# Gated mix of two attention blocks: the gate formed in the output's stage, mixed output weights stored one at a time, and five staging places for the second half of v

## The chip, the cores and the metric

The kernel runs on one core of one Trainium2 chip. The metric is device time in microseconds (us), the median of several runs of the whole program. TensorE is called PE, VectorE DVE, ScalarE ACT, GpSimd POOL; SP is the engine from whose queue this kernel issues all its DMAs, and the queue is worked off in the order in which the program was written.

## What is computed

One input x (2048 tokens of 1024) goes through two attention blocks with 32 heads of 32, and a gate per token mixes the results:

```python
g = sigmoid((x * gate_w).sum(-1, keepdims=True))
# A, linear attention: phi(t) = where(t > 0, t + 1, exp(t)) + 1e-6
kv = einsum("bhsd,bhse->bhde", phi(k), v); z = einsum("bhsd->bhd", phi(k))
a = (phi(q) kv / (phi(q) z + 1e-6)) @ A_wo
# B, softmax attention
b = softmax(q k^T * 32**-0.5) v @ B_wo
out = g * a + (1 - g) * b
```

All of it is in float32. A float32 product is made of three PE passes: each operand is split into a high part (a cast on ACT, L252) and a low part (a subtraction on DVE or POOL, L253), and high*high, high*low and low*high are added up in one PSUM bank (L146 to L148).

## The kernel before, in words

The program is written out by a planner. It keeps a modelled clock for each engine (`T`, advanced by `use`), several generators ("streams") that yield where they could go on, and a list of small DVE jobs that may be put off (`defer`, `fill`). At every step it takes the stream whose next work can start first or that is furthest behind. The instructions of each engine, and those of SP, then run on the chip in the order in which they were written; an engine waits wherever its next instruction has to.

There are 16 blocks of 128 tokens. The work comes in these stages:

- The first stage makes v's first half and all of B's q and k, and puts the parts of x away in DRAM (`xs`), from where blocks of x come back later.
- `linear()` then runs units of 24 matmuls, one unit for a block of tokens and 512 output columns: 16 units for v's second half ("v"), 64 for block A: keys and values ("kv", 64 units, 256 columns of each), then queries ("q") and outputs ("o") in 32 units each. Unit n reads x from one of two tiles, and the loads for unit n+2 (L583, two DMAs of 512 KB) are issued when unit n has ended.
- `maxima()` makes scores once for the row maxima (L902 on PE, L907 on DVE), beginning during v's second half; `heads_()` makes them again transposed, with the exponential (L1053 on PE, L1057 on ACT) and the sums with v (L1149). These two are interleaved with the units of `linear()`. All of them take their results from a ring of six PSUM banks.
- In stage "q" the keys' sums are multiplied into A's output weights (`mix()`, L669): four times, for two halves of the rows and two of the columns. `load_mix()` (L652) fetches four tiles of A's weights (1 MB) at units 2 and 8 of "q" and again of "o". A mix yields four results; each gives a high part (in the same four tiles, `mix_hi`, slices of `big12`) and a low part (`mix_lo`: `mid7`, `mid10`, `mid0`, `mid1`), and both go out to DRAM (`wa_d`, L679), eight DMAs of 256 KB. The destination of one such DMA is four pieces of 32 rows.
- `output()` takes B's weights and the finished heads, splits them (`split_o`), makes the last product block of tokens by block of tokens (`out_pe`), adds A's part `ra` and stores (`out_done`, L1227 and L1228). Tokens' results wait in a ring of five tiles, each with B's heads in its left half and `ra` in its right half. The last head's rows come into these tiles by five small DMAs (L1202) from `mid11`.

What the change touches: the gate is formed by `gate()` in the v units. For each block two DMAs bring x (L334) into quarters of `big20`, and two DVE instructions (L344) multiply them with the gate's weights (`zrep`, loaded by the program's first DMA, L329) and add them up; behind the last block five short instructions (L346 to L350) make g and 1-g of all blocks at once. g then multiplies the queries' results in `divide` (L824), and 1-g the output in `out_done`. `v_out` (L365 and L366) copies a v unit's bank on ACT into `mid10` or `mid11`, in turns, and stores it. In the first score pass, head 0 and head 1 of q, k and v are loaded in units 0 and 1 (`load_head`: L861, L873; `load_v`: L886).

Of the kernel before, what the change touches and what calls it, by code (L numbers as in the profile page):

```python
# [9 lines left out]
F32 = mybir.dt.float32  # L10
F32R = mybir.dt.float32r
AF = mybir.ActivationFunctionType
ALU = mybir.AluOpType
# [32 lines left out]
def kernel(  # L46
# [32 lines left out]
    def f32(ap):  # L79
        return ap.bitcast(F32)  # L80
# [28 lines left out]
    zrep = sb.tile([P, D], F32, name="zrep")  # L109
    g_sb = sb.tile([P, NT], F32, name="g_sb")  # L110
    omg_sb = sb.tile([P, NT], F32, name="omg_sb")
    tg = sb.tile([P, 2, NT], F32, name="tg")
    mx = [sb.tile([P, NT, NJ], F32, name=f"mx{i}") for i in range(2)]
    mneg = [sb.tile([P, NT], F32, name=f"mneg{i}") for i in range(2)]
    mh = sb.tile([NT, P], F32R, name="mh")
# [38 lines left out]
    def use(eng, cost, *after):  # L154

        T[eng] = max(T[eng], *after, 0.0) + cost
        return T[eng] + LATENCY[eng]
# [142 lines left out]
    PAIRS = [(j, j + 1) for j in range(0, NJ, 2)]  # L300
    tmp = f32(big[20])
    s1, u2, u3 = [tmp[:, i * C:(i + 1) * C] for i in range(3)]
    gate_x = [tmp[:, i * C:(i + 1) * C] for i in range(4)]

    def xop(name, p, i):
        return big[XO[name][p]][:, i * C:(i + 1) * C]
# [19 lines left out]
        nc.tensor.matmul(bank[7][:, :P], ones, ones, start=True, stop=True)  # L326

    HD = D // 2
    nc.sync.dma_start(zrep, bass.AP(tensor=gate_w.tensor, offset=gate_w.offset, ap=[[0, P], [1, D]]))  # L329

    def gate():
        def load(t):
            for i in range(2):
                nc.sync.dma_start(gate_x[t % 2 * 2 + i], x[t * P:(t + 1) * P, i * HD:(i + 1) * HD])  # L334

        load(0)
        for t in range(NT):
            yield
            if t + 1 < NT:
                load(t + 1)  # L340
            for i in range(2):
                gx = gate_x[t % 2 * 2 + i]
                use("dve", 0.7)
                nc.vector.scalar_tensor_tensor(gx, gx, 1.0, zrep[:, i * HD:(i + 1) * HD], op0=ALU.mult,  # L344
                                               op1=ALU.mult, accum_out=tg[:, i, t:t + 1])
        nc.vector.tensor_add(tg[:, 0], tg[:, 0], tg[:, 1])  # L346
        nc.scalar.activation(tg[:, 0], tg[:, 0], AF.Exp, scale=-1.0)
        nc.vector.tensor_scalar_add(tg[:, 0], tg[:, 0], 1.0)
        nc.vector.reciprocal(g_sb, tg[:, 0])
        nc.vector.tensor_scalar(omg_sb, g_sb, -1.0, 1.0, op0=ALU.mult, op1=ALU.add)  # L350

    def spill(js):

# [10 lines left out]
    def v_out(c, t, ps, va):  # L364
        nc.scalar.copy(va, ps)  # L365
        nc.sync.dma_start(v_d[c][:, t, :], va)  # L366
# [75 lines left out]
        nc.sync.dma_start(qk_d[sec][0][g][:, sl], f32(hi))  # L442
        nc.sync.dma_start(qk_d[sec][1][g][:, sl], f32(lo))

    gating = gate()
    xp_done = set()

    def first_xp(n):
# [197 lines left out]
    mixed = []  # L646
    mix_hi, mix_lo = [], (mid[7], mid[10], mid[0], mid[1])

    def load_mix():
        a, c = mix_todo.popleft()  # L650
        for i in range(HK):
            nc.sync.dma_start(mix_hi[i], a_wo[(a * HK + i) * P:(a * HK + i + 1) * P, c * C:(c + 1) * C])  # L652
        mix_here.append((a, c, T["pe"] + 8.0))
# [7 lines left out]
    def mix():  # L661
        a, c, _ = mix_here.pop()
        need(k_left)
        bs = [take() for _ in range(4)]
        end = use("pe", AV + 0.2)
        for r in range(4):
            rows = slice(r * DH, (r + 1) * DH)
            for i in range(HK):
                nc.tensor.matmul(bank[bs[r]][i * DH:(i + 1) * DH, :], kvb[rows, a * HK + i, :], mix_hi[i][rows, :],  # L669
                                 start=True, stop=True)  # L670
        for r in range(4):
            hi, lo, pb = f32r(mix_hi[r]), f32r(mix_lo[r]), bank[bs[r]]
            at = use("act", 0.5, end)
            nc.scalar.copy(hi, pb)

            def low(_, r=r, hi=hi, lo=lo, pb=pb):
                nc.vector.tensor_sub(lo, pb, f32(hi))
                for p, src in enumerate((hi, lo)):
                    nc.sync.dma_start(wa_d[p][a][c][:, r * DH:(r + 1) * DH, :], f32(src))  # L679
                mixed.append((a, c))  # L680

            give(bs[r], 0.0, [defer(low, at)])

# [37 lines left out]
    def linear():  # L721
        extra = iter(())
        coming_w = deque()
        for n, (i, t) in enumerate(units):
# [7 lines left out]
            ps = bank[b]  # L732
            T["pe"] = max(T["pe"], free[b])
            lin_kind[0] = kind
            if kind in ("q", "o") and c == 0 and t in (2, 8, NT - 2):
                yield lambda: None if mix_here else 0.0
                if t < NT - 2:
                    load_mix()
# [3 lines left out]
            for k in range(NK):  # L742
# [19 lines left out]
                if follow and follow[0] == "o":  # L762
                    if pos == NT - 1:
                        w_left[k].clear()
                        yield lambda: 0.0 if mixed.count((k // HK, follow[1])) == 4 else None
                        load_wa(follow[1], k)
                    continue
                if follow and pos == NT - 2 and k < min(LEAD_W, NK):
# [4 lines left out]
                        coming_w.append(load_w(*follow, k + LEAD_W, LEAD_W + 1))  # L773
            if NT // 2 <= n + 2 < len(units):
                load_xp(n + 2)
            for _ in range(1 + (n == 1) if n < NT else 0):
                next(gating, None)
            extra = iter(())
            e, r = mid[3 + n % 3], mid[6]
            if kind == "v":  # L780
                give(b, use("act", 0.5, T["pe"] + LATENCY["pe"]))
                v_out(c, t, ps, mid[10 + t % 2])
            elif kind == "kv":
                va = mid[7][:, (n % 2) * HC:(n % 2 + 1) * HC]
                yield from keys_alone(n - 2)
# [18 lines left out]
            elif kind == "q":  # L804
# [16 lines left out]

                def divide(_, t=t, e=e, ps=ps, d=d):
                    nc.vector.reciprocal(d, d)
                    nc.vector.scalar_tensor_tensor(  # L824
                        e.rearrange("p (h d) -> p h d", d=DH), ps.rearrange("p (h d) -> p h d", d=DH),
                        g_sb[:, t:t + 1], d.unsqueeze(2).to_broadcast([P, C // DH, DH]),
                        op0=ALU.mult, op1=ALU.mult)

                todo = chain(((sums, 0.63), (scaled, 0.63), (dens, 0.63), (divide, 0.9)), end)
                last.append(todo[-1])  # L830
# [187 lines left out]
    def heads_():  # L1018
# [8 lines left out]
        for h in range(H):  # L1027
# [6 lines left out]
            for t in range(NT):  # L1034
                i = slot(h, t)
                for j in range(NJ):
# [19 lines left out]
                    give(b, end)  # L1056
                    nc.scalar.activation(pr_t[i][:, j * C:(j + 1) * C], bank[b], AF.Exp, scale=SCALE)  # L1057
                    st_done[0] += 1
                    if j == 2 and t == 0 and h + 2 < H:
                        load_q(h + 2)  # L1060
                        load_v(h + 2)
# [142 lines left out]
    def split_o(n, ks):  # L1204
# [3 lines left out]
        xo_ready[n] = use("dve", 0.06 + 1.05 * size, use("act", 0.2 + 0.8 * size, T["pe"]))  # L1208
        split(blocks(dst, 0)[:, ks], blocks(dst, 1)[:, ks], o_part(n, ks), nc.vector)

    def out_pe(n, c, k):
        stat = [blocks(xo_t[n % len(xo_t)], p)[:, k] for p in range(2)]
        sl = slice(c * C, (c + 1) * C)
        if (n, c) not in out_b:
            out_b[n, c] = take()
        b = out_b[n, c]
        for _ in three(bank[b], stat, [wo_part(k, p)[:, sl] for p in range(2)], k):
            use("pe", MM, free[b])
# [13 lines left out]

    def output():
        yield lambda: None if "lin" in streams else 0.0
        early = list(range(min(5, NK - 1)))
        for k in early:
            for c in range(NQC):
# [3 lines left out]
        for n in range(1, NF):  # L1241
# [3 lines left out]
            for k in early:  # L1245
                for c in range(NQC):
                    yield lambda: both(wo_end[k], xo_ready[n], 0.0 if (n, c) in out_b else bank_at())
                    out_pe(n, c, k)
        for n in range(NF):
            for k in range(len(early), NK - 1):  # L1250
                for c in range(NQC):
                    yield lambda: wo_end[k]
                    out_pe(n, c, k)
# [10 lines left out]
        for n in range(NT):  # L1264
            if 2 < n + 1 < NT and n >= NF:
                split_o(n + 1, slice(0, NK))
            for c in range(NQC):
                for k in range(NK - 1 if n < NF else 0, NK):
                    out_pe(n, c, k)
                out_done(n, c)  # L1270
# [118 lines left out]
```

## Time and profile before

| | |
|---|---|
| Time, median of 3 runs | 2906.94 us (2906.63 to 2907.45) |
| The profiled execution's own time | 2906.63 us |
| Its span, first to last instruction | 2904.8 us |
| PE busy | 2847.1 us, 98% of the span |
| DVE, ACT, POOL busy | 2227.9, 1596.8 and 1853.9 us |
| Mean granted TensorE clock | 0.991 |
| DMA | 400.55 MB, mean 138 GB/s |

The span and the time differ by 1.8 us, which lie around the first and the last instruction. In the profile's rows, "x12" is a count, the number in front of it is busy time from the first to the last of the merged instructions, and a bracket such as "[6.37 <-DMA big<-xs]" is the idle time of that engine before the instruction and what ended it. "big<-xs" means that a tile called big (its number is left out) was written from xs. SPq is SP's queue: the time of its rows is that of issuing a DMA, not of the transfer. In rows of windows stand, for each engine, busy time and instruction count, then the granted clock, the mean busy share of the 16 DMA engines, and GB/s.

### The profile page before, as it was taken

What the parts mean: (1) busy time and instruction counts of PE and PEld (TensorE: products, weight loads), DVE (VectorE), ACT (ScalarE), POOL (GpSimd) and SP (SyncE); (2) the same over time, 40 slices, a digit from 0 to 9 for tenths busy, and PEclk for the clock granted to TensorE, in tenths of its full rate; (3) what the DMA queues carried; (4) which work ended last, traced back from release to release, by engine and by line L of the source; (5) the groups of instructions that cost most, each with busy time, mean ns of one, the idle gap of its engine ahead of it and who ended that gap; (6) DMA issues with size and microseconds to landing.
All of it is one profiled execution on the core that took longest, in us unless ns stands there. A gap on an engine that the chain in (4) does not pass through costs nothing.

```text
span 2904.8 us, 44336 instructions
## 1 busy us (share of the span) xinstructions
PE 2847.1 (98%) x15744; PEld 2039.5 (70%) x15744; DVE 2227.9 (77%) x3715; ACT 1596.8 (55%) x2976; POOL 1853.9 (64%) x646
## 2 busy tenths in 40 slices
PE   9999989899999999999999999799999999999999
PEld 7888867666666766666666666467676666766787
DVE  6667638788888888888888888688888887886522
ACT  5334320566676667666666666456666665666410
POOL 1212220488798889987988888468777878785000
PEclk9999999999999999999999999899999999999999
DMA  5957765423332324233323235444455344524542
GB/s 174 291 173 216 243 202 189 156 91 98 99 117 76 93 88 120 89 102 92 117 80 91 88 120 165 157 166 146 146 175 182 112 146 127 153 88 140 171 158 78
DMA packets 302496, 400.55 MB, mean 138 GB/s; under 512 B 92682, under 2 KB 185354, under 8 KB 299146
## 3 DMA queue, kind: packets, MB, share of 16 engines
q1 hardware_dynamic: 302276, 397.73, 44.3%
q8 instruction: 124, 2.03, 0.3%
q14 instruction: 96, 0.79, 0.1%
HBM read 287.57 MB, written 108.79 MB: 136 GB/s over the span
## 4 chain that ended last, share of the span: by engine, by line
PE 94%; DMA 3%; DVE 2%; ACT 0%; issue 0%; SPq 0%; ACTq 0%; DVEq 0%
PE bank L1053 16%; PE bank L902 16%; PE bank L1149 15%; PE bank L146 11%; PE bank L148 10%; PE bank L147 10%; PE bank L430 3%; PE bank L432 3%; PE bank L431 3%; PE bank L472 1%; PE bank L955 1%; PE bank L470 1%; PE bank L471 1%; DMA big<-xs 1%; DMA big<-qk 0%; PE bank L707 0%
## 5 line engine op out<-in xcount | busy, mean ns | idle before, releaser
L1102 POOL TENSOR_TENSOR big<-big,big 128x1536 f32<-128x1536 f32 (+1 forms) x434 | 1556.5, 3586 | 209.0 <-ACT big L1057 186.9
L907 DVE TENSOR_REDUCE mx<-bank 128x1 f32<-128x512 f32 x2048 | 1308.7, 680 | 306.7 <-PE bank L902 301.8
L1057 ACT ACTIVATE big<-bank 128x512 f32<-128x512 f32 x2048 | 1180.1, 601 | 528.1 <-PE bank L1053 457.8
L902 PE MATMUL bank<-big,big 128*128 128x512 f32 x2048 | 804.8, 393 | 21.6 <-DVE mx L907 11.9
L1053 PE MATMUL bank<-big,big 128*128 128x512 f32 x2048 | 810.7, 397 | 2.2 <-ACT big L1057 2.0
L146 PE MATMUL bank<-big,big 128*128 128x512 f32 x1408 | 554.6, 394 | 25.4 <-DMA big<-xs 21.4
L148 PE MATMUL bank<-big,big 128*128 128x512 f32 x1408 | 552.6, 392 | 1.0 <-DMA big<-oA 0.8
L147 PE MATMUL bank<-big,big 128*128 128x512 f32 x1408 | 552.8, 393 | 0.0
L1053 PEld LDWEIGHTS bank<-big,big 128*128 128x128 f32 x2048 | 384.4, 188 | 159.8 <-issue 62.8
L902 PEld LDWEIGHTS bank<-big,big 128*128 128x128 f32 x2048 | 385.9, 188 | 106.4 <-DVE mx L907 12.6
L1149 PE MATMUL bank<-big,mid 128*32 128x512 f32 x4096 | 459.2, 593 | 0.0
L146 PEld LDWEIGHTS bank<-big,big 128*128 128x128 f32 x1408 | 265.8, 189 | 91.2 <-issue 19.2
L1149 PEld LDWEIGHTS bank<-big,mid 128*32 128x32 f32 x4096 | 127.7, 110 | 263.6 <-issue 263.6
L148 PEld LDWEIGHTS bank<-big,big 128*128 128x128 f32 x1408 | 266.0, 189 | 58.5 <-DMA big<-oA 1.2
L147 PEld LDWEIGHTS bank<-big,big 128*128 128x128 f32 x1408 | 265.9, 189 | 55.4
L1111 DVE TENSOR_TENSOR bank<-bank,big 128x512 f32<-128x512 f32 (+1 forms) x434 | 280.2, 646 | 7.6 <-ACT big L1057 5.7
L1098 POOL TENSOR_TENSOR big<-big,big 128x1536 f32<-128x1536 f32 (+1 forms) x31 | 111.6, 3601 | 264.7 <-issue 141.1
L253 DVE TENSOR_TENSOR big<-mid,big 128x512 fp32r<-128x512 f32 x216 | 152.8, 731 | 83.9 <-ACT big L252 83.8
L409 POOL TENSOR_TENSOR mid<-mid,mid 128x512 f32<-128x512 f32 x16 | 20.7, 1291 | 278.3 <-DVE big L253 265.3
L252 ACT CAST big<-mid 128x512 fp32r<-128x512 f32 x216 | 130.2, 624 | 100.9 <-POOL mid L410 55.3
L431 PE MATMUL bank<-big,big 128*128 128x512 f32 x448 | 174.3, 389 | 0.0
L432 PE MATMUL bank<-big,big 128*128 128x512 f32 x448 | 174.3, 389 | 0.0
(102 smaller groups left out, 1949.8 us busy)
## 6 DMA issues: line engine op xcount, KB each, us to landing
big<-xs SPq DMA_DIRECT2D x208, 512.0 KB
qk<-mid SPq DMA_DIRECT2D x128, 256.0 KB
big<-oA SPq DMA_DIRECT2D x64, 512.0 KB
big<-qk SPq DMA_DIRECT2D x96, 256.0 KB
big<-qk SPq DMA_DIRECT2D x384, 64.0 KB
mid<-in_b_wqkv SPq DMA_DIRECT2D x88, 256.0 KB
xs<-big SPq DMA_DIRECT2D x64, 256.0 KB
oA<-mid SPq DMA_DIRECT2D x64, 256.0 KB
```

What stands on the lines that cost most here:

```text
L146: yield nc.tensor.matmul(ps, sh, mh_, start=(kt == 0), stop=False)
L147: yield nc.tensor.matmul(ps, sh, ml_, start=False, stop=False)
L148: yield nc.tensor.matmul(ps, sl, mh_, start=False, stop=(kt == NK - 1))
L431: nc.tensor.matmul(ps, sh, ml_, start=False, stop=False)
L432: nc.tensor.matmul(ps, sl, mh_, start=False, stop=(i == HK - 1))
L902: nc.tensor.matmul(bank[b], q[:, t * P:(t + 1) * P], k[:, j * C:(j + 1) * C], start=True, stop=True)
L907: nc.vector.tensor_reduce(m[:, t, j:j + 1], bank[b], AX.X, ALU.max)
L1053: nc.tensor.matmul(bank[b], k[:, t * P:(t + 1) * P], q[:, j * C:(j + 1) * C], start=True, stop=True)
L1057: nc.scalar.activation(pr_t[i][:, j * C:(j + 1) * C], bank[b], AF.Exp, scale=SCALE)
L1102: nc.gpsimd.tensor_add(lacc[:, :qp], lacc[:, :qp], pr(t)[:, :qp])
L1111: nc.vector.tensor_add(lacc[:, qp:] if t == NT - 1 else l_b[:, :n], l_b[:, :n], src)
L1149: nc.tensor.matmul(av_b[j * DH:(j + 1) * DH, :], v[:, t, :], pr(t)[:, j * C:(j + 1) * C], start=(t == 0), stop=(t == NT - 1))
```

## The change

The gate's stage is gone from the v units. `load_g` and a new `gate(n)` stand in `output()`: x of blocks 0 and 1 is loaded when `linear()` has ended, into `mid8`, `mid9` and `mid7`, `mid10`, the gate's weights ahead of them into `zrep` (which block A has used for something else in between), and `gate(n)` loads x of block n+2 behind its own products. It makes g and 1-g of one block in six short DVE and ACT instructions and multiplies `ra` by g on ACT, over 1024 columns; `divide` no longer multiplies by g. Blocks 0 and 1 are gated ahead of the middle part of the output's products, each later block n+1 ahead of block n's products.

`mix()` in stage "q" no longer issues its eight stores at once: they are put into a queue, `stores`, and `heads_()` issues one at each step of four transposed scores (at j == 1). Whatever is left goes out at once when the next `load_mix()` comes or stage "o" begins. In stage "o" the stores are issued as before. `mixed` now counts eight stores instead of four pairs.

`v_out` uses five tiles in turns, `mid10`, `mid11`, `mid7`, `mid8`, `mid9`.

```diff
-    nc.sync.dma_start(zrep, bass.AP(tensor=gate_w.tensor, offset=gate_w.offset, ap=[[0, P], [1, D]]))
-
-    def gate():
-        def load(t):
-            for i in range(2):
-                nc.sync.dma_start(gate_x[t % 2 * 2 + i], x[t * P:(t + 1) * P, i * HD:(i + 1) * HD])
...
+    stores = deque()
+
     def load_mix():
+        while stores:
+            stores.popleft()()
         a, c = mix_todo.popleft()
...
-            def low(_, r=r, hi=hi, lo=lo, pb=pb):
+            def store(p, src, r=r):
+                nc.sync.dma_start(wa_d[p][a][c][:, r * DH:(r + 1) * DH, :], f32(src))
+                mixed.append((a, c))
+
+            def low(_, hi=hi, lo=lo, pb=pb, store=store):
                 nc.vector.tensor_sub(lo, pb, f32(hi))
                 for p, src in enumerate((hi, lo)):
-                    nc.sync.dma_start(wa_d[p][a][c][:, r * DH:(r + 1) * DH, :], f32(src))
-                mixed.append((a, c))
+                    if lin_kind[0] == "q":
+                        stores.append(lambda p=p, src=src: store(p, src))
+                    else:
+                        store(p, src)
...
+            while kind == "o" and stores:
+                stores.popleft()()
...
-            for _ in range(1 + (n == 1) if n < NT else 0):
-                next(gating, None)
...
-                v_out(c, t, ps, mid[10 + t % 2])
+                v_out(c, t, ps, mid[(10, 11, 7, 8, 9)[n % 5]])
...
-                    nc.vector.scalar_tensor_tensor(
+                    nc.vector.tensor_mul(
                         e.rearrange("p (h d) -> p h d", d=DH), ps.rearrange("p (h d) -> p h d", d=DH),
-                        g_sb[:, t:t + 1], d.unsqueeze(2).to_broadcast([P, C // DH, DH]),
-                        op0=ALU.mult, op1=ALU.mult)
+                        d.unsqueeze(2).to_broadcast([P, C // DH, DH]))
...
+                    if j == 1 and stores:
+                        stores.popleft()()
...
+    gate_x = [(mid[8], mid[9]), (mid[7], mid[10])]
+
+    def load_g(n):
+        if n == 0:
+            nc.sync.dma_start(zrep, bass.AP(tensor=gate_w.tensor, offset=gate_w.offset, ap=[[0, P], [1, D]]))
+        t = t_order[n]
+        for i in range(2):
+            nc.sync.dma_start(gate_x[n % 2][i], x[t * P:(t + 1) * P, i * HD:(i + 1) * HD])
+
+    def gate(n):
+
+        t = t_order[n]
+        g, o = g_sb[:, t:t + 1], omg_sb[:, t:t + 1]
+        for i in range(2):
+            gx = gate_x[n % 2][i]
+            nc.vector.scalar_tensor_tensor(gx, gx, 1.0, zrep[:, i * HD:(i + 1) * HD], op0=ALU.mult,
+                                           op1=ALU.mult, accum_out=tg[:, t, i:i + 1])
+        nc.vector.tensor_add(g, tg[:, t, 0:1], tg[:, t, 1:2])
+        nc.scalar.activation(g, g, AF.Exp, scale=-1.0)
+        nc.vector.tensor_scalar_add(g, g, 1.0)
+        nc.vector.reciprocal(g, g)
+        nc.vector.tensor_scalar(o, g, -1.0, 1.0, op0=ALU.mult, op1=ALU.add)
+        ra = o_ring[n % len(o_ring)][:, D:2 * D]
+        nc.scalar.activation(ra, ra, AF.Copy, scale=g)
+        use("act", 1.4, use("dve", 2.2))
+        if n + 2 < NT:
+            load_g(n + 2)
...
         yield lambda: None if "lin" in streams else 0.0
+        for n in range(NF):
+            load_g(n)
...
         for n in range(NF):
+            gate(n)
...
                 split_o(n + 1, slice(0, NK))
+            if NF <= n + 1 < NT:
+                gate(n + 1)
```

Three places of the order are looked at below. Names are tiles with the number of the buffer: `bank` is PSUM, `mx0` the row maxima, `tg` the gate's sums, `wa` the mixed weights in DRAM, `oA` block A's results in DRAM; a first number says which of several a tile is.

On DVE, where the score maxima begin in v's second half, before:

```order
L253 TENSOR_TENSOR big19_227<-mid13_242,big19_227 128x512
L344 SCALAR_TENSOR_TENSOR big20_228,tg_199<-big20_228,zrep_196 128x512 x6
L907 TENSOR_REDUCE mx0_200<-bank5_248 128x1
L907 TENSOR_REDUCE mx0_200<-bank6_249 128x1
L907 TENSOR_REDUCE mx0_200<-bank0_243 128x1
L907 TENSOR_REDUCE mx0_200<-bank1_244 128x1
```

The same place now:

```order
L253 TENSOR_TENSOR big19_227<-mid13_242,big19_227 128x512
L892 TENSOR_REDUCE mx0_200<-bank5_248 128x1
L892 TENSOR_REDUCE mx0_200<-bank6_249 128x1
L892 TENSOR_REDUCE mx0_200<-bank0_243 128x1
L892 TENSOR_REDUCE mx0_200<-bank1_244 128x1
```

The six products of the gate that stood ahead of the first maximum are gone from there.

On SP, around the second mix of stage "q" (the loads of x for unit 9, the results of unit 6, then the fetch of A's weights), before:

```order
L583 DMA big5_213<-xs0_9_72 128x1024
L583 DMA big5_213<-xs1_9_88 128x1024
L714 DMA oA0_6_101<-mid8_237 128x512
L714 DMA oA1_6_117<-mid9_238 128x512
L652 DMA big12_3828<-in_a_wo 128x512 x4
```

The same place now:

```order
L559 DMA big5_213<-xs0_9_72 128x1024
L559 DMA big5_213<-xs1_9_88 128x1024
L700 DMA oA0_6_101<-mid8_237 128x512
L700 DMA oA1_6_117<-mid9_238 128x512
L657 DMA wa1_0_0_166<-mid0_229 4x32x512
L657 DMA wa0_0_0_162<-big12_3758 4x32x512
L657 DMA wa1_0_0_166<-mid1_230 4x32x512
L632 DMA big12_3758<-in_a_wo 128x512 x4
```

The last three stores of the first mix, which before went out in one piece with the other five, ahead of the loads of x for unit 8, are now right ahead of the second fetch; the second of the three reads the quarter of `big12` that the fetch's last DMA writes.

On SP, ahead of the last head's five small DMAs in the output's stage, now (before, the first five of these rows were not there):

```order
L1202 DMA zrep_196<-in_gate_w 128x1024
L1205 DMA mid8_237<-in_x 128x512
L1205 DMA mid9_238<-in_x 128x512
L1205 DMA mid7_236<-in_x 128x512
L1205 DMA mid10_239<-in_x 128x512
L1171 DMA big8_3751<-oB_127 128x896
L1172 DMA big8_3751<-ra1_171 128x1024
L1184 DMA big8_3751<-oB_127 96x128
L1189 DMA big12_3758<-mid11_240 32x128
```

The gate's weights and x of two blocks, 1.5 MB, now go ahead of the loads of the fifth block and of the last head's rows.

More of the change, by code (lines that the diff above doesn't have):

```diff
@@ L111 @@
     omg_sb = sb.tile([P, NT], F32, name="omg_sb")
-    tg = sb.tile([P, 2, NT], F32, name="tg")
+    tg = sb.tile([P, NT, 2], F32, name="tg")
     mx = [sb.tile([P, NT, NJ], F32, name=f"mx{i}") for i in range(2)]
@@ L302 @@
     s1, u2, u3 = [tmp[:, i * C:(i + 1) * C] for i in range(3)]
-    gate_x = [tmp[:, i * C:(i + 1) * C] for i in range(4)]
     def xop(name, p, i):
@@ L328 @@
     HD = D // 2
-    nc.sync.dma_start(zrep, bass.AP(tensor=gate_w.tensor, offset=gate_w.offset, ap=[[0, P], [1, D]]))
-    def gate():
-        def load(t):
-            for i in range(2):
[L334 to L350, printed above, removed]
     def spill(js):
@@ L443, in qk_out @@
         nc.sync.dma_start(qk_d[sec][1][g][:, sl], f32(lo))
-    gating = gate()
     xp_done = set()
@@ L764, in linear @@
                         w_left[k].clear()
-                        yield lambda: 0.0 if mixed.count((k // HK, follow[1])) == 4 else None
+                        yield lambda: 0.0 if mixed.count((k // HK, follow[1])) == 8 else None
                         load_wa(follow[1], k)
```

## The prediction

> **What bounds the kernel now.** The page comes first: how busy PE is, and what runs beside it.
>
> ```profile
> PE 2847.1 (98%) x15744; PEld 2039.5 (70%) x15744; DVE 2227.9 (77%) x3715; ACT 1596.8 (55%) x2976; POOL 1853.9 (64%) x646
> ```
>
> PE is busy in all but 57.7 us of the span of 2904.8. As the change takes no matmul away, it can win back only what PE waits, and what it loses behind a wait by a slow clock. So the next view is PE's waits, by what ended them:
>
> ```profile
> PE bank L146 <- DMA big<-xs: 21.4, 2, 15.0
> PE bank L902 <- DVE mx L907: 11.9, 1, 11.9
> PE bank L902 <- ACT mid L365: 9.5, 2, 6.8
> PE bank L470 <- ACT big L252: 2.5, 1, 2.5
> PE bank L146 <- DVE big L573: 2.1, 1, 2.1
> ```
>
> Few, long waits, 47.4 us in five rows. The first row is two waits for x in stage "q" (6.4 and 15.0), the second and a part of the third (9.5 - 6.8 = 2.7) lie where v's second half begins, the other part (6.8) and the fifth at its end. The windows right behind these waits show the second loss, the granted clock (the number behind the last engine's count):
>
> ```profile
> 424.50:426.60 2.10, 2.04 (x4) 1.16 (x4) 0.00 (x0) 0.01 (x1) 0.00 (x0) 0.50 0.96 218
> 438.50:446.50 8.00, 8.00 (x29) 6.55 (x30) 7.33 (x14) 0.58 (x1) 0.00 (x0) 0.81 0.66 214
> 534.20:542.20 8.00, 8.00 (x29) 6.52 (x30) 6.01 (x11) 4.58 (x9) 0.85 (x1) 0.82 0.83 164
> 1843.90:1851.90 8.00, 8.00 (x30) 5.34 (x34) 4.75 (x9) 3.06 (x5) 4.45 (x2) 0.76 0.99 335
> 1887.90:1895.90 8.00, 8.00 (x29) 6.51 (x30) 4.90 (x8) 2.58 (x5) 0.00 (x0) 0.73 0.58 212
> ```
>
> A window's length times what is missing to 1.00 is time lost: 1.1, 1.5, 1.4, 1.9 and 2.2 us.
>
> **The change part by part.** *The gate leaves the v units: the first wait goes.* SP's queue, DVE and ACT at the beginning of v's second half (timeline):
>
> ```profile
> 420.07 0.38 SPq L366 DMA_DIRECT2D v<-mid  x1
> 421.91 7.76 SPq L873 DMA_DIRECT2D big<-qk  x12
> 430.38 2.70 SPq L334 DMA_DIRECT2D big<-in_x  x4
> 434.85 0.69 DVE L344 SCALAR_TENSOR_TENSOR big<-big,zrep 128x512 f32<-128x512 f32 x1 [11.07 <-DMA big<-in_x]
> 437.75 4.40 DVE L907 TENSOR_REDUCE mx<-bank 128x1 f32<-128x512 f32 x7
> 423.92 0.58 ACT L365 COPY mid<-bank 128x512 f32<-128x512 f32 x1 [11.35 <-DMA v<-mid]
> ```
>
> x for the gate is queued on SP behind the twelve loads of head 1's k, so it lands late; DVE stands 11.07 us before the gate's product at 434.85, the maxima stand behind it until 437.75, seven in a row, and PE has no bank left. Now the maxima follow directly (first pair of listings of the order). Their operands are not late: no wait of PE for head 0's loads is among its rows. The 2.7 us ahead of it is another queue: ACT's third copy waited 11.35 us for the first store of v, which SP issued at 420.07, behind head 0's loads; with five places the third copy needs no store to have landed. The three new places' last use, B's stores of q and k, stands on SP ahead of head 0's loads. I see nothing that is late next: the whole of 11.9 + 2.7 + 1.1 + 1.5 = **17.2 us** goes. The gate's DVE products, removed with it, lay on no other path.
>
> *The end of v's second half.*
>
> ```profile
> 512.69 7.24 SPq L260 DMA_DIRECT2D mid<-in_a_wqkv  x10
> 521.29 0.81 SPq L334 DMA_DIRECT2D big<-in_x  x2
> 522.80 4.54 SPq L260 DMA_DIRECT2D mid<-in_a_wqkv  x6
> 529.16 2.06 ACT L571 CAST big<-mid 128x512 fp32r<-128x512 f32 x3 [4.93 <-DMA mid<-in_a_wqkv]
> 533.41 0.22 ACT L347 ACTIVATE tg<-tg 128x16 f32<-128x16 f32 x1 [2.19 <-DVE tg L346]
> 534.15 0.79 PE L902 MATMUL bank<-big,big 128*128 128x512 f32 x1 [6.85 <-ACT mid L365]
> 520.00:530.00 10.00, 5.17 (x22) 3.64 (x20) 3.65 (x6) 3.23 (x7) 0.00 (x0) 1.00 0.99 327
> ```
>
> PE waits for block A's weights (2.1), then for a bank that ACT empties only behind the casts of three more weights and the gate's exponential. The exponential's 2.2 us wait goes. The casts wait for weights from transfers that run at 327 GB/s with the engines 0.99 busy; two gate loads of 0.5 MB less ahead of them are 3.1 us at that rate. Together 5.3 of the 9.0 us, and most of the clock's 1.4, are taken as **6.5 us**; the bounds are 2.2 (the transfers' end does not move) and 10.3 (everything).
>
> *The stores one at a time: both waits for x go.*
>
> ```profile
> 1822.00:1829.00 7.00, 7.00 (x32) 5.68 (x31) 5.76 (x12) 5.03 (x9) 6.92 (x2) 1.00 0.27 104
> 1819.30 2.61 SPq L679 DMA_DIRECT2D wa<-big  x1
> 1827.02 2.46 SPq L679 DMA_DIRECT2D wa<-mid  x1
> 1835.75 2.70 SPq L583 DMA_DIRECT2D big<-xs  x2
> 1868.13 2.40 SPq L679 DMA_DIRECT2D wa<-mid  x1
> 1881.61 4.59 SPq L583 DMA_DIRECT2D big<-xs  x4
> ```
>
> From the fifth store on, each holds SP for about 2.5 us, while the DMA engines are 0.27 busy: about four of sixteen carry them. Behind eight of them x for unit 8 is issued at 1835.75 and for unit 10 at 1881.61, where PE had stopped 9 us before. Now three stores lie between unit 7's and unit 8's loads, and single ones elsewhere. x lands some 6 us behind its issue (1881.61 to PE's start at 1887.8, ahead of the fifth window), and a unit of "q" lasts longer than that. So 21.4 + 1.9 + 2.2 = **25.5 us** go; were each load still held up by a store in front, about half would stay, the lower bound 13.
>
> The Trainium skill, "DMA: Bandwidth & Descriptors", section "Rules for kernel authors", says that a DMA whose outermost dimension has size c below 16 runs on at most c DMA engines; this store's has four, and the 0.27 agrees. By that rule spreading the stores out makes none of them shorter, and its section "Queues, rings and completion order" adds that each engine takes its descriptors in order, so a load issued behind a store still waits on those four; that outcome is the third rival.
>
> *A new wait at the second mix.* The second pair of listings of the order has three stores right ahead of the fetch of A's weights. Before, that fetch had a free queue:
>
> ```profile
> 1843.85 0.77 PE L146 MATMUL bank<-big,big 128*128 128x512 f32 x1 [6.37 <-DMA big<-xs]
> 1854.66 1.16 PE L669 MATMUL bank<-big,kvb 32*32 32x512 f32 x32
> ```
>
> PE begins unit 8 at 1843.85 and the mix at 1854.66, 10.8 us later, 8.9 at full clock; the order of PE's work there is unchanged. Now, counted from unit 8's start: x of unit 9 and results of unit 6, 1.5 MB at 335 GB/s, with some 1 us of issue, end at 5.7; three stores of 2.5 us on the same four engines at 13.2; 1 MB of weights behind them, 3.1 us, at 16.3. PE would wait 16.3 - 8.9 = 7.4 us, and lose about 2 by the clock, as behind the wait of 6.4: **9.5 us lost**. The bounds are 0 (the stores overlap the rest) and 12.
>
> *The gate in the output's stage.*
>
> ```profile
> L344 DVE SCALAR_TENSOR_TENSOR big<-big,zrep 128x512 f32<-128x512 f32 x32 | 20.9, 686 | 29.3 <-DMA big<-in_x 29.1
> L252 ACT CAST big<-big 128x1024 fp32r<-128x1024 f32 (+2 forms) x18 | 16.8, 956 | 117.4 <-PE bank L147 91.0 <-DMA big<-mid 26.3
> 2760.00:2780.00 20.00, 20.00 (x90) 16.57 (x89) 4.78 (x6) 2.11 (x2) 0.00 (x0) 1.00 0.55 177
> 2733.68 4.48 SPq L1202 DMA_DIRECT2D big<-mid  x5
> 2739.97 2.40 ACT L252 CAST big<-big 128x128 fp32r<-128x128 f32 x4 [14.13 <-DMA big<-mid]
> 2746.59 2.11 DVE L1227 SCALAR_TENSOR_TENSOR big<-bank,omg_sb,big 128x512 f32<-128x512 f32 x3 [3.91 <-PE bank L148]
> 2724.00:2740.00 16.00, 15.16 (x59) 12.05 (x60) 7.46 (x11) 1.87 (x4) 0.00 (x0) 0.89 0.62 216
> ```
>
> Each block costs DVE two products of 0.69 and four short instructions (estimate 0.8 in all), ACT the exponential's 0.22 and a scaling near the cast's 0.96, and 0.5 MB. A block is 48 matmuls, 10.7 us at 90 in 20 us; in that window DVE is busy for a quarter and ACT for a tenth, so these are hidden, also the wait of DVE for ACT within them, since ring and banks run blocks ahead. The first blocks are tighter: 1.5 MB now precede the last head's rows on SP, 7 us at 216 GB/s. They landed at 2739.97; their casts and subtractions take 0.9, and PE came to them at about 2745.7 (its first result is taken at 2746.59): 4.8 us of slack. **1 us lost** (between 0 and 4).
>
> *The program's start.* SP's first DMA was the gate's weights:
>
> ```profile
> 0.75 0.39 SPq L329 DMA_DIRECT2D zrep<-in_gate_w  x1
> ```
>
> Its issue, 0.4, and a part of its 0.5 MB go: **0.7 us** (0 to 2) of the 2.5 that PE waits for its first operands.
>
> The sum is -17.2 - 6.5 - 25.5 + 9.5 + 1.0 - 0.7 = -39.4 us, against the profiled execution's 2906.6: 2867. That execution lies 0.3 below the median of the three runs, which changes nothing.
>
> **The rivals.**
>
> *No new wait at the second mix.* If the stores drain beside the loads, or the fetch's data wait only for the one store that reads their place, the 9.5 stay: 2858. For it: the fetch before was never waited for at this place. Against it: the 0.27. Chance 0.27.
>
> *Spread stores still hold up x.* Half of the 25.5 stays: 2867 + 13 = 2880. For it: each store takes 2.5 us wherever it is. Against it: a unit leaves more than that. Chance 0.14.
>
> *Slower.* The output's stage could become bound by transfers. A block moves 1.5 MB now (heads, `ra`, result) and 2.0 MB with x. Did this stage get no more than the 138 GB/s that the page has as mean, a block would take 14.8 instead of 10.7 us, and 14 blocks 57 us more: 2867 + 57 = 2924. It decides from 2.0 MB in 10.7 us on, 190 GB/s. Against it: engines only 0.55 busy at 177 GB/s here and 335 GB/s elsewhere. Chance 0.03.
>
> *The change doesn't do what it says* can be left out: the order shows all three edits.
>
> **How the numbers follow.** The forecast has 0.56, the rivals 0.27, 0.14 and 0.03. The time is that of the likeliest, 2867. The range goes down past the second case with all of the end of v's half won (2858 - 3.8, about 2854) and up past the third, with some of the output's bound (2880 + 3): 2854 to 2883. Faster by over 0.2% (5.8 us, about what a measurement of this kernel can tell) is every case but the last; the smallest sum of the lower gains, 17.2 + 2.2 + 13 - 12 - 4 = 16 us, is faster too. 0.95 faster, 0.02 the same, 0.03 slower.
>
> **What would show it.** Among PE's waits: no DVE mx at the first maxima, no DMA big<-xs of over 2 us; ACT's copies of v without a wait for v's stores; at the end of v's half one wait of about 3.5 us; at the second mix a wait of PE for big<-in_a_wo of about 7 us; none by DMA big<-in_x in the output's stage. A time under 2854 would mean that the mix and the end of v's half both cost nothing; over 2883, that waits for x stay in "q", or that new ones came where the order had none.

## The result and the profile after

The changed kernel takes 2873.41 us (median of four runs, 2870.82 to 2873.77) against 2907.19 before (four runs, 2906.63 to 2909.41). The ratio is 0.988, with a 95% interval of 0.9863 to 0.9898: 33.8 us faster. The forecast was 39.4 us. The profiled execution took 2873.77 us, with a span of 2872.0, 32.8 less than before. All that follows is compared with that profiled execution.

The page of the changed kernel, PE and the engines beside it:

```profile
PE 2846.1 (99%) x15744; PEld 2036.8 (71%) x15744; DVE 2239.1 (78%) x3775; ACT 1617.8 (56%) x3007; POOL 1854.1 (65%) x646
```

PE's busy time is the same within 1.0 us. Outside it there are 25.9 us of the span where there were 57.7. So 31.8 of the 32.8 us are waits that went. Only 1.0 is shorter busy time, in which a better clock would show; the forecast had a net 5.8 there. PE's waits after the change, to be held against the five rows of the prediction:

```profile
PE bank L649 <- DMA big<-in_a_wo: 7.5, 1, 7.5
PE bank L146 <- DMA big<-xs: 3.4, 2, 2.0
PE bank L887 <- ACT mid L342: 2.9, 1, 2.9
PE bank L1038 <- ACT big L1042: 2.6, 1, 2.6
PE bank L146 <- ACT big L252: 1.9, 1, 1.9
PE bank L446 <- ACT big L252: 0.8, 1, 0.8
```

The 11.9 us for a maximum (DVE mx) are gone, the two waits for x fell from 21.4 to 3.4, and the two for ACT's copies of v (now L342) from 9.5 to 2.9. The first row is the wait at the second mix. It was forecast at 7.4. SP's queue shows how it comes about (after, timeline):

```profile
1814.04 0.51 SPq L657 DMA_DIRECT2D wa<-mid  x1
1814.61 0.64 SPq L657 DMA_DIRECT2D wa<-big  x1
1815.29 1.82 SPq L657 DMA_DIRECT2D wa<-mid  x1
1817.15 8.91 SPq L632 DMA_DIRECT2D big<-in_a_wo  x4
```

The three stores left over from the first mix stand ahead of the fetch of A's weights, as the order had shown. SP then needs 8.91 us to issue four loads.

What that wait costs in all is seen on PE, before and then after, from the mix (L669, now L649) to the four transposes (L707, now L693):

```profile
1855.75 1.93 PE L1149 MATMUL bank<-big,mid 128*32 128x512 f32 x16
1857.60 0.66 PE L707 MATMUL bank<-ident,mid 128*128 128x128 f32 x4
```

```profile
1829.48 3.79 PE L649 MATMUL bank<-big,kvb 32*32 32x512 f32 x32 [7.53 <-DMA big<-in_a_wo]
1833.20 3.17 PE L1136 MATMUL bank<-big,mid 128*32 128x512 f32 x16
1836.31 0.66 PE L693 MATMUL bank<-ident,mid 128*128 128x128 f32 x4
```

Before, the mix began at 1854.66 and the transposes 2.9 us later. Now they begin 6.8 us after the mix's start, with the same matmuls between. So the second mix costs 7.5 of wait and 3.9 behind it, 11.4 us. These 3.9 lie inside "busy" rows: the row of the mix, 32 matmuls of 0.6 us merged, took 1.16 before and takes 3.79 now, and shows no wait among them.

The windows behind the waits, and one of the output's stage (after):

```profile
509.00:516.00 7.00, 7.00 (x19) 5.53 (x20) 5.44 (x10) 3.89 (x7) 0.00 (x0) 0.59 0.98 202
1829.50:1837.50 8.00, 8.00 (x56) 2.41 (x57) 2.48 (x4) 3.10 (x7) 0.00 (x0) 0.61 0.11 25
1853.50:1859.50 6.00, 5.95 (x28) 5.02 (x29) 4.47 (x7) 2.90 (x6) 3.69 (x1) 1.00 0.66 230
1920.40:1926.40 6.00, 5.97 (x31) 2.60 (x35) 5.00 (x9) 3.72 (x7) 4.70 (x2) 0.72 0.94 317
2760.00:2780.00 20.00, 20.00 (x90) 16.56 (x89) 8.35 (x22) 4.59 (x6) 0.00 (x0) 1.00 0.65 210
```

Length times what is missing to 1.00 gives 2.9, 3.1, 0, 1.7 and 0 us. The last row is the stage that took over the gate: PE is busy in all of the 20 us, while DVE went from 4.78 to 8.35, ACT from 2.11 to 4.59 and the transfers from 177 to 210 GB/s. The gate is hidden there.

### The profile page after: what moved, and what is told of

Read it like the earlier page. It is cut to its first block, busy times and chain, and to the rows that moved or that the text cites. A ratio compares the mean times of both kernels' runs of the same rounds, so it can differ in the third digit from the quotient of the medians.

```text
span 2872.0 us, 44436 instructions
## 1 busy us (share of the span) xinstructions
PE 2846.1 (99%) x15744; PEld 2036.8 (71%) x15744; DVE 2239.1 (78%) x3775; ACT 1617.8 (56%) x3007; POOL 1854.1 (65%) x646
## 4 chain that ended last, share of the span: by engine, by line
PE 96%; DMA 2%; DVE 1%; ACT 0%; issue 0%; SPq 0%; ACTq 0%; DVEq 0%
PE bank L1038 16%; PE bank L887 16%; PE bank L1136 15%; PE bank L146 11%; PE bank L148 11%; PE bank L147 11%; PE bank L407 4%; PE bank L409 4%; PE bank L408 4%; PE bank L446 1%; PE bank L940 1%; PE bank L447 1%; PE bank L448 1%; DMA big<-xs 1%; PE bank L693 0%; PE bank L584 0%
## 5 line engine op out<-in xcount | busy, mean ns | idle before, releaser
L1038 PE MATMUL bank<-big,big 128*128 128x512 f32 x2048 | 810.7, 397 | 2.7 <-ACT big L1042 2.6
L1038 PEld LDWEIGHTS bank<-big,big 128*128 128x128 f32 x2048 | 384.6, 188 | 159.7 <-issue 62.0
```

Of the source, the lines that this page charges most:

```text
L1038: nc.tensor.matmul(bank[b], k[:, t * P:(t + 1) * P], q[:, j * C:(j + 1) * C], start=True, stop=True)
```

## The experiments

The theory was that the gains are separate (gate, v's places, stores) and that the new wait at the second mix comes from the stores ahead of the fetch. The rivals were that the gains hide one another, and that not the place of the stores holds up the loads behind them but their form, four pieces on four DMA engines. Each run is compared with the kernel before on the same chip; ratios come with their 95% interval.

**The gate alone.** The changed kernel with its stores and v's places as before:

```diff
-                    if lin_kind[0] == "q":
+                    if False:
...
-                v_out(c, t, ps, mid[(10, 11, 7, 8, 9)[n % 5]])
+                v_out(c, t, ps, mid[10 + t % 2])
```

> The change with only the gate moved: v's copies take two places, the mixed weights' stores go out eight at a time as before. Theory (the gate's products hold up the first maxima, and its loads the end of v's second half): PE's waits by DVE mx (11.9 us) and most of the end of v's half go, with some clock; PE waits by big<-xs in stage q stay at about 21 us; the 2.7 us by ACT's copy stay or shrink. Time 2884 to 2890 us. Rival (the places of v and the stores carry the gain): under 8 us gained, 2899 or more.

Measured: 2884.97 us against 2907.10, ratio 0.9924 (0.9909 to 0.9939). PE's waits in it:

```profile
PE bank L146 <- DMA big<-xs: 21.5, 2, 15.1
PE bank L887 <- ACT mid L342: 4.9, 2, 3.1
```

The time is in the theory's range. The waits for x are untouched and there is none at the mix. The gate is worth 22 us by itself. It wins at the first maxima, where 1.9 of the second row remain, and also at the end of v's half, where its larger wait, 3.1, is what remains.

**The stores alone.** The kernel before with the queue of stores (`mix()`, `load_mix()`, `heads_()` and the emptying at stage "o" as in the diff above; the main lines):

```diff
                 for p, src in enumerate((hi, lo)):
-                    nc.sync.dma_start(wa_d[p][a][c][:, r * DH:(r + 1) * DH, :], f32(src))
-                mixed.append((a, c))
+                    if lin_kind[0] == "q":
+                        stores.append(lambda p=p, src=src: store(p, src))
+                    else:
+                        store(p, src)
...
+                    if j == 1 and stores:
+                        stores.popleft()()
```

> The kernel before with only the stores of stage q issued one at a time. Theory: the two waits for x of 21.4 us and 4 us of slow clock behind them shrink to about 3.4 us, and the wait of 7.5 us at the second mix, with 3 us of slow clock, comes up as it does in the full change: 2894 to 2898 us. Rival (the new wait belongs to the moved gate or to its timing, not to the stores): no wait at the mix, 2884 to 2887 us.

Measured: 2897.79 us against 2907.10, ratio 0.9969 (0.9956 to 0.9982). Its waits:

```profile
PE bank L914 <- DVE mx L919: 12.9, 1, 12.9
PE bank L673 <- DMA big<-in_a_wo: 8.6, 2, 8.3
PE bank L146 <- DMA big<-xs: 4.5, 2, 2.6
```

The time is in the theory's range. The wait for `in_a_wo` appears with the stores and without the gate, so it belongs to them. The gate's own waits stand in this kernel as before. The stores win 16.9 us of waits for x and pay 8.3 at the mix; 9.3 us are left in the medians.

**The five places alone.** The kernel before with one line changed:

```diff
-                v_out(c, t, ps, mid[10 + t % 2])
+                v_out(c, t, ps, mid[(10, 11, 7, 8, 9)[n % 5]])
```

> The kernel before with only five places for v's copies. Theory: ACT's wait of 11.35 us for v's first store goes, but PE gains nothing, since the maxima still stand behind the gate's product and release PE's banks at the same moment: 2905 to 2908 us. Rival (the 2.7 us that ACT ended are a gain of their own): 2903 to 2904.5 us.

Measured: 2908.77 us against 2907.10, ratio 1.0005 (0.9995 to 1.0015): no gain, 0.8 us above the theory's range. Its waits show why:

```profile
PE bank L902 <- DVE mx L907: 14.7, 1, 14.7
PE bank L902 <- ACT mid L365: 5.2, 1, 5.2
```

The wait of 2.7 ahead of the first maxima went, and the one behind it grew from 11.9 to 14.7. As long as DVE stands before the gate's product, freeing ACT earlier only lets PE reach the same wall sooner. At the end of v's half the 9.0 us of before (6.8 and 2.1) became 8.6: the 5.2 of the second row and a new wait for x of 3.4.

**The change without the five places:**

```diff
-                v_out(c, t, ps, mid[(10, 11, 7, 8, 9)[n % 5]])
+                v_out(c, t, ps, mid[10 + t % 2])
```

> The full change with two places for v's copies, as before. Theory: with the gate gone, ACT's wait for v's first store is no longer covered by a longer one, and PE waits about 2 us for ACT at the first maxima (1.9 us in the run with only the gate moved): 2874.5 to 2877 us. Rival: the places are worth nothing even then, 2872.5 to 2874 us.

Measured: 2875.44 us against 2908.80, ratio 0.99 (0.987 to 0.9931). Its four times range from 2873.56 to 2892.98 us, too wide to settle 2 us by time, though the median is in the theory's range. The waits show them:

```profile
PE bank L887 <- ACT mid L342: 4.8, 2, 2.8
```

This is the 2.9 of the changed kernel's row and one more wait of 2.0 that ends at 430.3, at the first maxima. With the gate gone the places take away about 2 us of waiting; the forecast had 2.7.

**Two stores at each step.** If only the three stores ahead of the fetch cost, sending them out earlier should win the mix back:

```diff
-                    if j == 1 and stores:
+                    if j % 2 and stores:
```

> The full change with two stores for each step of four scores instead of one, so that all eight of the first mix are out before the second fetch; PE's order is the same. Theory (the new wait at the second mix comes from the three stores that go out right ahead of the fetch): the 7.5 us and about 3 us of slow clock behind them go, 2862 to 2866 us; the waits for x stay at about 3 us. Rival (the fetch is late by itself, since it is issued only at unit 8's start, behind x of unit 9 and the results of unit 6): the wait at the mix stays at 5 us or more, 2870 to 2874 us.

Measured: 2873.85 us against 2907.10, ratio 0.9886 (0.9872 to 0.9901), the same as the change. The theory missed, and the time is the rival's. Its waits, and SP behind the second mix:

```profile
PE bank L649 <- DMA big<-in_a_wo: 4.3, 1, 4.3
PE bank L146 <- DMA big<-xs: 4.0, 3, 3.1
```

```profile
1845.84 4.45 SPq L657 DMA_DIRECT2D wa<-mid  x1
1850.34 2.65 SPq L657 DMA_DIRECT2D wa<-big  x1
1853.09 2.80 SPq L559 DMA_DIRECT2D big<-xs  x2
```

No store stands between the loads of x and the fetch any more, and the mix's wait fell from 7.5 to 4.3 only; the last two stores of the first mix now go out just ahead of those loads (at 1809.39 and 1810.01). Behind the mix the stores, now denser, hold SP for 4.45 and 2.65 us right ahead of x for a later unit. What a store holds up moves with it.

**Each store as four DMAs.** This tests the form of the store. It writes the same bytes to the same places in four DMAs of 32 rows, the rest is the changed kernel:

```diff
-                nc.sync.dma_start(wa_d[p][a][c][:, r * DH:(r + 1) * DH, :], f32(src))
+                for i in range(HK):
+                    nc.sync.dma_start(wa_d[p][a][c][i, r * DH:(r + 1) * DH, :], f32(src)[i * DH:(i + 1) * DH, :])
```

> The full change with each store of the mixed weights cut into four DMAs of 32 rows, 64 KB each, the same bytes. Theory (a store whose destination has four pieces runs on four of the sixteen DMA engines, and loads issued behind it stand on those four): the waits for x in stage q fall from 3.4 to under 1.5 us, SP never takes over 2 us for one piece, and the wait at the second mix falls from 7.5 us to 3 to 5, since the fetch still stands behind 12 issues of 0.4 to 0.5 us: 2863 to 2868 us. Rival (only the order on SP counts, and more DMAs make it worse): the wait at the mix stays at 7 us or more, 2872 to 2877 us.

Measured: 2861.08 us against 2908.80, ratio 0.9836 (0.9819 to 0.9852), 12 us below the change. SP at the second mix, PE there, and the waits:

```profile
1814.30 2.75 SPq L658 DMA_DIRECT2D wa<-big  x4
1817.10 1.83 SPq L658 DMA_DIRECT2D wa<-mid  x4
1818.97 1.88 SPq L632 DMA_DIRECT2D big<-in_a_wo  x4
```

```profile
1822.00 4.99 PE L649 MATMUL bank<-big,kvb 32*32 32x512 f32 x32 [2.91 <-DMA big<-in_a_wo]
```

```profile
PE bank L649 <- DMA big<-in_a_wo: 2.9, 1, 2.9
PE bank L888 <- ACT mid L342: 2.8, 1, 2.8
PE bank L1039 <- ACT big L1043: 2.0, 1, 2.0
```

The gain is larger than the theory's: the time lies below its range. Four times as many DMAs, yet the fetch behind the stores is issued in 1.88 us instead of 8.91, the mix waits 2.9 instead of 7.5, and no wait for x is left. The Trainium skill, "DMA: Bandwidth & Descriptors", section "Rules for kernel authors", says that a DMA whose outermost dimension has size c below 16 runs on at most c engines. The 3.4 us of waits for x and 4.6 of the 7.5 that went when four pieces became four DMAs of 32 rows agree with it. Each DMA also became smaller, 64 KB for 256; no run varies that alone.

**All pieces at once.** The same four DMAs per store, but issued together as before the change. It tells the form from the spreading:

```diff
-                    if lin_kind[0] == "q":
+                    if False:
```

> The full change with the stores of stage q in pieces of 32 rows as in the run with wide stores, but all at once as in the kernel before, 32 DMAs in a row. Theory (both count: four busy DMA engines, and SP, which is held for 0.45 us by each of 32 issues): x for the units behind each mix is still issued some 14 us late, but lands faster; waits for x of 8 to 16 us in place of the 21 that the eight narrow stores gave, and no wait at the second mix: 2866 to 2874 us. Rival (the width alone is the cause): no wait for x over 2 us, 2856 to 2861 us. Second rival (the burst on SP alone is the cause): waits for x of 20 us or more, 2876 us or more.

Measured: 2870.02 us against 2907.83, ratio 0.9867 (0.9853 to 0.9882). PE's largest wait, and SP (eight rows of four pieces between 1825.70 and 1840.89, the last of them first here, then the loads of x behind them):

```profile
PE bank L146 <- DMA big<-xs: 11.8, 3, 9.6
```

```profile
1839.09 1.80 SPq L658 DMA_DIRECT2D wa<-mid  x4
...
1844.79 4.54 SPq L559 DMA_DIRECT2D big<-xs  x4
```

The theory came true in its time and in both waits. While these stores go out, the DMA engines are twice as busy as in the prediction's window for the stores in four pieces (0.27 busy at 104 GB/s):

```profile
1826.00:1833.00 7.00, 7.00 (x38) 5.27 (x31) 6.49 (x11) 5.58 (x12) 0.00 (x0) 1.00 0.51 127
```

That is more than four engines at work. SP is not freed sooner: these 32 DMAs hold it for 15.2 us, the eight of before held it for 13.5 (the first of them below, the last ended at 1829.48).

```profile
1816.01 0.60 SPq L679 DMA_DIRECT2D wa<-big  x1
```

With the two kernels above this makes a table of two by two, all four with the gate moved (the first with two places for v):

| PE waits for x + at the mix, time | stores at once | one at a time |
|---|---|---|
| four pieces in one DMA | 21.5 + 0, 2885.0 us | 3.4 + 7.5, 2873.4 us |
| four DMAs of 32 rows | 11.8 + 0, 2870.0 us | 0 + 2.9, 2861.1 us |

Both the form and the spreading count. The form is worth 15 us with the stores at once (less the 2 of v's places) and 12 us with them spread. The 2861.1 us were measured on another chip than the two times of the first column; the medians of the kernel before differ by up to 1.7 us between these runs.

**The mix later.** The planner is told that the fetched weights come later, so that it puts the mix further back in PE's order:

```diff
-        mix_here.append((a, c, T["pe"] + 8.0))
+        mix_here.append((a, c, T["pe"] + 18.0))
```

> The full change with the planner told that a mix's weights take 18 us from their fetch instead of 8: the second mix moves back by about two units of stage q, the others by one; the stores stay as they are. Theory (PE's wait at the mix is only the fetch's landing behind three stores, and nothing else needs the mix that early): no wait for big<-in_a_wo, no slow clock there, 2861 to 2866 us, with waits for x of 2 to 5 us as before. Rival (the lost time moves on: waits for x grow once PE no longer pauses there): 2869 to 2874 us.

Measured: 2870.74 us against 2908.80, ratio 0.9873 (0.9858 to 0.9888), 3 us below the change in medians, with intervals that overlap, and not the 7 to 12 of the theory. Its waits:

```profile
PE bank L1038 <- DMA big<-ml: 4.5, 1, 4.5
PE bank L1038 <- ACT mid L822: 3.8, 1, 3.8
PE bank L903 <- ACT mid L822: 3.3, 1, 3.3
PE bank L887 <- ACT mid L342: 3.0, 1, 3.0
```

The wait for `in_a_wo` is gone, but the two mixes of stage "o" moved too, and three new waits of 11.6 us stand in that stage, where stores still go out at once; that the stores cause them was not tried. The rival's number came true, by another mechanism than it named: its waits for x did not grow.

**Three casts later as well.** To the last kernel, the casts of the last three of block A's first weights are put behind ACT's copy of v's last unit:

```diff
+        casts = deque()
...
-                    split_w(*follow, k, *coming_w.popleft(), nc.vector if kind == "v" else nc.gpsimd)
+                    raw = coming_w.popleft()
+                    if kind == "v" and k >= LEAD_W:
+                        casts.append((k, raw))
+                    else:
+                        split_w(*follow, k, *raw, nc.vector if kind == "v" else nc.gpsimd)
...
+                while casts:
+                    k, raw = casts.popleft()
+                    split_w(*follow, k, *raw, nc.vector)
```

> As the run with the later mixes, and at the end of v's half the casts of the last three weight tiles stand behind ACT's copy of the last v unit instead of ahead of it. Theory (the 2.9 us there are ACT's copy behind casts that wait for weights, and the 6.8 us of half clock come from that wait): the wait by ACT's copy goes, a shorter one for the weights themselves comes, 2 to 5.5 us less than with the later mixes alone: 2857 to 2863 us. Rival (PE needs those weights at the same moment): the same time as with the later mixes alone.

Measured: 2868.25 us against 2908.80, ratio 0.9862 (0.9847 to 0.9876). The wait for ACT's copy of v, 3.0 in the row above, is gone. In its place PE waits a little later for the exponentials behind the casts:

```profile
PE bank L1046 <- ACT big L1050: 1.7, 1, 1.7
```

It is 2.5 us below the kernel without it in medians, the low end of what the theory took off; by the ratios' intervals that is not certain, though the four times of each do not overlap (2866.39 to 2869.49 against 2869.76 to 2874.43). The 2857 to 2863 us did not come, as they stood on the missed forecast for the later mixes. The clock has no part in the gain: it is 1.00 from 509 to 516 in both kernels. That the last copy of v waited behind casts is shown by the wait that went.

**Together.** Four DMAs per store, two stores at each step and the casts later:

> The full change with wide stores, two of them for each step of four scores, and the last three casts of block A's weights behind ACT's copy of the last v unit. Theory (what is left of the second mix's wait, 2.9 us with 1.7 to 3 of slow clock, is the three stores' 12 issues ahead of the fetch; the end of v's half gives 1 to 4 us): 2852 to 2858 us, the wait by big<-in_a_wo under 1 us. Rival (the fetch's own landing is the rest, and the casts only change what PE waits for): 2859 to 2862 us.

Measured: 2859.43 us against 2907.83, ratio 0.9834 (0.9818 to 0.9851), 14 us below the change.

```profile
PE bank L1047 <- ACT big L1051: 4.3, 3, 1.9
PE bank L649 <- DMA big<-in_a_wo: 1.4, 1, 1.4
```

That is not told apart by time from the kernel with the four DMAs alone (2861.08), and the wait at the mix did not fall under 1 us: the theory missed, and the time is in the rival's range. Priced as above, from the wait's start to the four transposes, the second mix still costs 5.4 us here (transposes at 1829.63) and 7.3 with the four DMAs alone (at 1829.33), against 11.4 in the change. Those two are the fastest kernels of the study.

## Why the forecast was right, and where its sizes were off

- **The gate at the first maxima (17.2): right.** Both waits went, and with them the clock's loss. The waits of the two kernels with one part each show the working's order: the gate was the wall, v's places only count behind it (0 without the gate moved, about 2 with).
- **The end of v's half (6.5): right in its waits, wrong in its clock.** 9.0 us became 2.9, against 3.7 forecast to remain. But "most of the clock's 1.4" was not won: 2.9 us are lost in the window at 509, behind a wait a third as long. Net 6.1 - 1.5 = 4.6. That loss is this execution's own. In six more kernels that wait is 2.8 to 3.1 us; in the 7 us behind it 1.5 to 1.7 us are lost in three (the gate alone, two stores at each step, all pieces at once) and nothing in the other three (two places for v, four DMAs per store, the later mixes).
- **Gate and places together.** The gate's terms without v's 2.7 come to -20.7 (-17.2 + 2.7 - 6.5 + 1.0 - 0.7), and the kernel with the gate alone measured -22.1.
- **The waits for x (25.5): mostly right.** 18.0 of 21.4 went. "A unit of q lasts longer than that" holds where one store stands ahead of a load, not where several stand close together: 2.0 us stay at 1853.5 and 1.4 at 1881.9. The rival that half stays was right in kind, at a small part of its size; its mechanism, the store's form, is borne out by the run with four DMAs one at a time, where nothing stays.
- **The second mix (9.5): the wait right, partly by luck, and what follows it short.** The wait was 7.5 against 7.4. Counted from unit 8's first product, at 1812.97, it ends after 16.5 us, where the forecast had 16.3. That stores ahead of the fetch cause it is shown: with the gate alone and with all pieces at once, where the first mix's stores go out together and SP is done with them more than 6 us ahead of the fetch, the mix does not wait. But the forecast put 7.5 of its 16.3 us down to the three stores right ahead. With two stores at each step these are gone from there, and PE still goes on only after 13.9 us (1812.27 to 1826.12), not after 8.8. So taking them from that place is worth 2.6 of the 7.5. Stores further ahead hold up the fetch too, which the sum did not have: with the same order and four DMAs per store (the last kernel above) PE goes on after 10.4 us (1812.30 to 1822.72). What lies behind the wait was 3.9 and not 2: 3.1 of half clock in the window at 1829.5, and about 0.8 of pauses among the mix's first matmuls (5 of the 32 are at work in the first 1.4 us, to 1830.9). 11.4 us in all, still inside the bound of 12. The likeliest rival (no new wait) was wrong.
- **The stores as a whole.** This is the step that was mis-sized: -25.5 + 9.5 = -16.0 forecast; the stores alone measured -9.3 (interval -12.8 to -5.2), and put onto the gate -11.6 with v's places. The missing part, in the profiles, is 3.4 of waits for x, 1.9 behind the mix, and a wait at 1917.8 for ACT's exponentials (L1038) that grew from 2.0 to 2.6 us and now loses 1.7 by the clock. That wait's size changes from kernel to kernel (none with the gate alone, 1.0 with the stores alone, 2.0 with the four DMAs); what sets it was not tried.
- **The output's stage (1.0 lost): nothing was lost.** No wait for x or for the last head's rows came, and the fourth case (transfers bind the stage) was far: 210 GB/s, engines 0.65 busy.
- **The start (0.7): more.** The wait for the first operands fell from 2.5 to 0.8.

Two gains of the clock were not in the sum; the windows of before at the start and at the last block of the output show them:

```profile
6.00:12.00 6.00, 4.76 (x13) 3.53 (x14) 5.30 (x8) 4.23 (x7) 0.00 (x0) 0.72 0.77 287
2724.50:2730.50 6.00, 5.66 (x17) 4.18 (x18) 5.76 (x8) 1.34 (x3) 0.00 (x0) 0.72 0.50 156
```

Each lost 1.7 us, and the granted clock of the same places after is 1.00. Neither gain is shown to be the change's. With the stores alone, where the gate's weights are still the first load, the clock from 6 to 12 is 1.00 too; with four DMAs per store, where the gate is in the output's stage, 0.81 stands behind the wait at the last block (2679 to 2688), again 1.7 us. So these 3.4 us can't be counted on. The 6.6 us between forecast (39.4) and profile (32.8) split into 1.8 of waits and 4.8 of busy time. Of the busy time, by the rows above: 2.7 at the end of v's half (2.9 lost where the sum left about 0.2), 1.9 behind the mix, 1.7 at 1920, less 3.4 for these two windows, make 2.9. About 2 us I could not place.

## What to carry to other kernels

When several waits follow each other on the critical engine, the work queued in front of the last one decides; freeing an earlier one gains nothing until that is moved. Before spreading slow DMAs out in a queue, look at why they are slow: a store whose destination falls into few pieces delayed what was issued behind it in every order tried here, and cutting it into DMAs of many rows won 12 to 15 us, where spreading the stores won 9 to 12. Price a wait with what follows it, the slow clock and the pauses inside merged rows, by reading the time from the wait's start to the next known instruction in both traces. Do not read the clock behind a short wait out of one profile as the change's doing: look for the same wait in another kernel.

## What the runs showed of the hardware

A wait's length does not tell whether the clock falls. After waits of 2.9 and 2.6 us PE ran at 0.59 and 0.72 for 7 and 6 us; after one of 2.0 (at 1853.5) it kept 1.00; before the change 1.8 us (at 2724.5) were enough for 0.72, while the 1.9 at the same place after cost nothing. The clearest pair is the end of v's half in the changed kernel and in the one with the later mixes, whose edit acts only in later stages. The wait is 2.9 us in the one, with 0.59 behind it, and 3.0 in the other, with this behind it:

```profile
509.60:516.60 7.00, 6.97 (x30) 5.56 (x31) 7.00 (x13) 5.95 (x11) 2.41 (x1) 1.00 1.04 211
```

What decides between the two, no run here shows. The Trainium skill, "TensorE: Matmul & The Clock Gate", section "Why this matters for your kernels", asks for no idle gaps over about 3 us; here gaps of 1.8 to 2.9 us already cost 1.7 to 2.9 us in some cases, so the measurement decides against that bound as a safe one.

A store in four pieces can hold SP's queue for 2.4 to 4.5 us where several are under way; issued alone it mostly takes 0.5 to 0.7. The four DMAs of 32 rows that replace it mostly take 1.8 us together, and at the most 4.69 (at 1834.54 in the run with four DMAs one at a time). So cutting the store up did not make its own issue shorter, 15.2 us against 13.5 for the eight at once. It made what stood behind the stores come sooner: the fetch was issued in 1.88 us instead of 8.91, and of 21.5 us of waits for x 11.8 were left with the stores at once.
